# A fused attention and MLP kernel: attention of tiles 0 to 6 moved ahead of the first products with w_in

## The chip, the cores and the metric

The kernel runs on one core of a Trainium2 chip. The time is that of one execution on the device in microseconds (us); for a kernel several runs are taken and their median is given. Four engines compute: TensorE (PE in the profile, its weight loads PEld), VectorE (DVE), ScalarE (ACT) and GpSimd (POOL). SyncE (SP) only issues transfers. POOL issues those transfers that convert float32 to bfloat16 on the way.

## The reference

Attention with a band of 96 keys and 8 global keys, over 4 batches, 8 heads, 768 positions and a head size of 64; then an MLP with a squared ReLU on its 3072 rows of 512:

```python
scores = scale * np.matmul(q, k.transpose(0, 1, 3, 2))
is_global = pos[None, :] < n_global                  # 8
is_local = (rel >= 0) & (rel < n_local)              # 96
scores = scores - slopes * dist                      # per head
scores = np.where(is_global | is_local, scores, -1000000000.0)
a = np.exp(scores - np.max(scores, axis=-1, keepdims=True))
a = a / (np.sum(a, axis=-1, keepdims=True) + 1e-09)
x = np.matmul(a, v)                                  # heads joined: 3072 x 512
h = x @ w_in                                         # 512 x 2048
g = np.maximum(h, 0.0) ** 2
return g @ w_out                                     # 2048 x 512
```

## The kernel before

**Tiles.** The 3072 rows are 24 tiles of 128, six to a batch. A query tile needs its own keys, those of the tile before, and the 8 global keys of its batch; the first tile of a batch (0, 6, 12, 18) needs only its own. Two tiles make a pair, or block; the MLP runs by blocks, 12 of them.

**Steps of a tile**, by the names that the order uses; the line is where most of a step's work is issued:

- `ld` or `load`: POOL's transfers of q, k and v. `gate` is a tiny write ahead of a load into a buffer used before.
- `tr`: PE transposes q (n = 0) or k (n = 1), line 506; `T`: a copy of that from PSUM to `qkT`. From tile 8 on a transposing DMA on SP's queue does both, and is then called `T` alone.
- `bias`: for tiles 0 to 2, PE adds the position bias, line 579. `sc`: the scores, line 599.
- `exp`: ScalarE's exponential, line 665; `mul`: VectorE multiplies by E, the exponential of the bias, from tile 3 on, line 690. For a batch's first tile it is E0, made on VectorE in two halves.
- `gk`, `gv`: the 8 global keys or values are copied beside a tile's own; `kl` is a copy of keys that serves instead of `gk` for some tiles. The next tile needs them.
- `pv`: the product with v, line 748, in two halves of four heads; `norm`: VectorE's reciprocal and scaling, lines 778 and 779.
- `trx`: PE transposes x, line 816; `xT`: the copy of that. From tile 8 on both are one transposing DMA.

**The MLP.** Blocks 0 and 1 compute h step by step (`s1`, line 1061): 256 of the 2048 hidden columns in a step, each followed by `relu` and `sq`. Step s needs the transfer `win.s`; steps 0 and 2 come in two halves. Block 0's product with w_out is `s2.0` (line 1339). All other products are done with seven half-size products in the place of eight: `h` (line 950) and `s2` (line 1212), whose sums of operands VectorE makes (`isum`, `xs`, `wsum`, `sum`), and whose parts ScalarE and VectorE copy out and add (`u`, `c`, `q`, `part`, `o`). `u` is a copy of a partial result, in one of four buffers.

**What sets the order.** The kernel builds a list of all steps, with what each depends on, and a table of words, ORDER, gives the order in which they are issued. Every engine runs its own instructions strictly in that order. In a word, `@V`, `@A` and `@P` choose VectorE, ScalarE or POOL, the digits behind a colon name the PSUM banks (there are eight), and `#2` is the second piece of a step. The table is all that decides the order: the planner's estimates that stand in the code are not used when it runs.

**The start.** PE first runs eight products of zeros (line 372), then ORDER begins. Its second word is `warm`: eight more products of zeros, line 532, between the two transposes of tile 0:

```python
            def emit_warm(e):
                for _ in range(NKEEP):
                    nc.tensor.matmul(out=psum(), lhsT=zero[:, :P], rhs=zero, start=True, stop=True)
```

Tile 0's q and k come as float32 by SP; POOL loads the rest. In ORDER's first rows attention of tiles 0 to 3 comes ahead of the first `s1`; that of tiles 4 and 5 is spread among the products of blocks 0 and 1, and tile 6 follows after the first `h`.

Of the kernel before, what the change touches and what calls it, by code (L numbers as in the profile page):

```python
# [62 lines left out]
exp.3.0.1 T.1.4@V xT.1@V pv.2.1:0 ld.k.5 ld.win.2.0 exp.3.1.1 gk.3@A ld.win.2.1 norm.2.0 s1.0.3:2 mul.3.0 s1.0.6:4
ld.win.4.0 tr.0.4:7 ld.q.5 ld.v.4 norm.2.1 mul.3.1 relu.0.6@A s1.0.3#2 gv.2@P pv.3.0:3 norm.3.0 trx.2:5 T.0.4@A
pv.3.1:6 ld.win.1.0 norm.3.1 ld.win.0.1 xT.2@A sc.4.0:1047 exp.4.1.1 exp.4.1.0 tr.1.5:3 T.1.5@A s1.0.2:5 trx.3:6
xT.3@V ld.win.0.0 ld.win.5.0 s1.0.2#2 s1.0.2#3 s1.0.2#4 relu.0.3@V exp.4.0.1 ld.v.5 gv.3@P exp.4.0.0 gk.4@V sq.0.6@V
relu.0.2@A s1.1.3:7 ld.win.7.0 relu.1.3@A load.6 s1.1.6:0 mul.4.1 tr.0.5:6 mul.4.0 sq.0.3@V s1.1.2:3 T.0.5@A ld.wout.3
# [10 lines left out]
isum.1.0 T.8 s2.0.6.1 u.2.1.2@A s2.0.6.0 isum.3.0 pv.6.1:0 h.2.0.p6 wsum.2.1 wsum.0.1 s2.1.p1.1 s2.0.7.1 c.2.1.c11
norm.6.0 gate.13 o.0.1@V st.0.1 s2.0.7.0 h.2.1.p7 part.1.p1@A s2.1.p6.0 u.2.0.2@A o.0.0@A u.2.1.3@A h.2.0.p7 h.2.1.p4
T.9 norm.6.1 wsum.3.0 u.2.0.3@A sc.7.0:1762 c.2.1.c21@A wsum.1.1 h.2.1.p5:0 c.2.1.c22 q.2.1.c11@A s2.1.p2.0:4  # L80
exp.7.1.0 exp.7.0.0 isum.2.1 load.10 h.2.0.p4 exp.7.0.1 mul.7.0 exp.7.1.1 s2.1.p2.1 isum.2.0 s2.2.p1.0:7 q.2.1.c21@A
mul.7.1 h.2.0.p5:1 s2.1.p6.1 part.1.p6@A trx.6:6 gate.12 c.2.0.c21@A load.12 pv.7.0:2 xT.6@A c.2.0.c22 q.2.1.c22@A
q.2.0.c22@A s2.2.p1.1 h.2.1.p3 s2.1.p7.0 wsum.3.1 o.1.p2 norm.7.0 h.2.0.p3 pv.7.1:5 s2.1.p7.1 q.2.0.c21@A st.0.0
c.2.1.c12 s2.1.p5.0 s2.1.p5.1 part.1.p7@A q.2.1.c12@A s2.1.p4.0 T.10 s2.1.p4.1 c.2.0.c12 gk.7@V q.2.0.c12@A o.1.p5
o.1.p4@A sc.8.0:6201 st.1.1 part.2.p1@A s2.1.p3.0 norm.7.1 sum.2.0 sum.2.1 s2.1.p3.1 trx.7:5 xT.7@V o.1.p3 h.3.0.p1:3
exp.8.1.0 gk.8@V h.3.1.p1:2 exp.8.0.0 exp.8.1.1 exp.8.0.1 h.3.0.p2:6 xs.3.0 u.3.1.1@A sc.9.0:1540 s2.2.p6.0 mul.8.0
xs.3.1 mul.8.1 u.3.0.1@A h.3.0.p6 exp.9.0.1 exp.9.1.1 gv.7@V h.3.1.p2:4 c.3.0.c11 h.3.1.p6 c.3.1.c11 exp.9.0.0
pv.8.0:0 s2.2.p6.1 pv.8.1:6 load.11 norm.8.0 u.3.1.2@A s2.2.p2.0:1 sum.2.2 gv.8@P q.3.1.c11@A norm.8.1 xT.8 h.3.1.p7
h.3.0.p5:4 u.3.0.2@A h.3.0.p7 s2.2.p2.1 exp.9.1.0 st.1.0 part.2.p6@A xs.3.2 u.3.1.3@A q.3.0.c11@A h.3.1.p5:0 s2.2.p7.0
u.3.0.3@A mul.9.1 mul.9.0 s2.2.p7.1 c.3.1.c22 T.12 c.3.0.c22 pv.9.0:6 h.3.1.p3 o.2.p2 h.3.0.p4 c.3.1.c12 load.15  # L90
norm.9.0 q.3.1.c22@A h.3.0.p3 s2.3.p1.0:5 s2.3.p1.1 c.3.0.c12 q.3.0.c22@A pv.9.1:0 c.3.0.c21@A part.2.p7@A norm.9.1
q.3.1.c12@A h.3.1.p4 q.3.0.c12@A h.4.0.p1:3 c.3.1.c21@A s2.2.p5.0 part.3.p1@A gk.9@V sc.10.0:6402 s2.2.p5.1
q.3.0.c21@A sum.3.0 sum.3.1 s2.2.p4.0 s2.2.p4.1 exp.10.1.0 sum.2.3 exp.10.0.0 exp.10.0.1 h.4.0.p2:4 T.11 u.4.0.1@A
exp.10.1.1 gk.10@V gv.9@A s2.3.p6.0 o.2.p5 mul.10.0 c.4.0.c11 xT.9 h.4.1.p1:6 o.2.p4@A mul.10.1 s2.2.p3.0 s2.2.p3.1
q.3.1.c21@A s2.3.p2.0:0 sum.3.2 u.4.1.1@A pv.10.0:2 pv.10.1:4 s2.3.p6.1 xs.4.0 gate.17 o.2.p3 part.3.p6@A xs.4.1
s2.3.p2.1 norm.10.0 h.4.0.p6 h.4.1.p6 q.4.0.c11@A gv.10@A norm.10.1 u.4.0.2@A load.13 s2.3.p7.0 sc.11.0:7124 u.4.1.2@A
sum.3.3 h.4.0.p7 h.4.1.p7 xs.4.2 exp.11.1.0 o.3.p2 exp.11.0.0 u.4.0.3@V s2.3.p7.1 sc.12.0:17 exp.11.1.1 exp.11.0.1
gate.16 xT.10 h.4.0.p4 c.4.0.c21@A mul.11.0 st.2.0 mul.11.1 h.4.1.p2:4 c.4.1.c11 exp.12.1.0 s2.3.p5.0 pv.11.0:2
pv.11.1:3 s2.3.p5.1 norm.11.0 part.3.p7@A h.4.0.p5:7 q.4.1.c11@A u.4.1.3@A norm.11.1 h.4.1.p5:4 q.4.0.c21@A gate.20
s2.3.p4.0 c.4.0.c22 load.14 s2.3.p4.1 h.4.0.p3 T.13 gate.18 load.16 c.4.1.c22 exp.12.0.0 h.4.1.p4 q.4.1.c22@A h.4.1.p3  # L100
xT.11 s2.4.p2.0:2 h.5.0.p1:3 q.4.0.c22@A o.3.p5 mul.12.0 c.4.0.c12 o.3.p4@A c.4.1.c21@A u.5.0.1@A c.4.1.c12 T.15
s2.3.p3.0 q.4.0.c12@A s2.3.p3.1 q.4.1.c12@V q.4.1.c21@A h.5.0.p2:1 o.3.p3 sc.13.0:5764 st.3.1 st.2.1 h.5.1.p1:0
exp.13.0.0 T.14 s2.4.p2.1 c.5.0.c11 exp.13.1.0 pv.12.1:1 q.5.0.c11@A s2.4.p1.0:5 xs.5.0 sum.4.0 pv.12.0:7 xs.5.1
s2.4.p1.1 mul.13.0 h.5.0.p6 gk.13@V u.5.1.1@A exp.13.0.1 h.5.1.p6 exp.13.1.1 h.5.0.p5:6 sum.4.1 norm.12.0 norm.12.1
h.5.1.p2:4 xs.5.2 mul.13.1 c.5.1.c11 h.5.1.p5:7 u.5.1.2@A sum.4.2 gate.19 part.4.p1@A h.5.1.p7 u.5.0.2@A h.5.0.p7
o.4.p2 u.5.0.3@A c.5.0.c22 pv.13.0:1 u.5.1.3@A norm.13.0 s2.4.p6.0 s2.4.p6.1 xT.12 st.3.0 q.5.1.c11@A T.16 part.4.p6@A
h.5.0.p4 pv.13.1:4 s2.4.p5.0 sum.4.3 c.5.0.c21@A h.5.0.p3 h.5.1.p4 q.5.0.c22@A s2.4.p7.0 norm.13.1 s2.4.p7.1 s2.4.p5.1
c.5.0.c12 q.5.0.c21@A kl.15@V part.4.p7@A c.5.1.c22 q.5.0.c12@A sc.14.0:1346 o.4.p5 s2.4.p4.0 xT.13 exp.14.0.1 kl.14@V
h.5.1.p3 gv.13@P q.5.1.c22@V c.5.1.c12 c.5.1.c21@A s2.4.p4.1 load.17 h.6.0.p1:4 s2.4.p3.0 s2.4.p3.1 exp.14.1.1
exp.14.1.0 exp.14.0.0 sc.15.0:0673 mul.14.1 mul.14.0 xs.6.0 o.4.p4@A xs.6.1 h.6.0.p2:1 o.4.p3 q.5.1.c12@A s2.5.p1.0:5  # L110
u.6.0.1@A c.6.0.c11 exp.15.0.0 exp.15.1.0 exp.15.1.1 sum.5.0 s2.5.p1.1 h.6.0.p6 u.6.0.2@A exp.15.0.1 sum.5.1 load.18
h.6.0.p5:2 part.5.p1@A pv.14.0:0 norm.14.0 pv.14.1:6 h.6.1.p1:1 u.6.1.1@A h.6.0.p7 gv.14@P st.4.0 s2.5.p6.0 u.6.0.3@A
# [52 lines left out]
def kernel(  # L165
# [119 lines left out]
    HALVES = ((NBLK - 2, 0), (NBLK - 2, 1))  # L285
# [1146 lines left out]
```

## Time and profile before

| | |
|---|---|
| runs | 199.08, 199.46, 200.98 us; median 199.46 |
| profiled execution | 198.44 us, of which its span, first to last instruction, is 196.7 |
| PE busy | 190.8 us, 97% of the span, 2776 matmuls |
| VectorE, ScalarE, POOL busy | 173.9 (88%), 162.9 (83%), 80.9 (41%) |
| granted TensorE clock | 0.998 |

The profile records one execution. A row of a timeline gives start, length, engine, line and operands; of the chain of waits, start, length and what was running on the chain that ended last. A stretch's row gives the stretch, then the busy time of PE, PEld, DVE, ACT and POOL in it with the number of instructions, then the granted clock, the transfers' share and their rate. Lines of groups give busy time, mean length of one and idle time before.

Matmuls overlap, and so do other instructions at their ends; where one follows the other without a pause, the time from start to start is what an instruction costs its engine.

### The profile page before, as it was taken

The numbers are of one execution on the slowest core, as the hardware profiler recorded it, in microseconds if no ns is written. First come the engines' busy times: TensorE is split into PE (matmuls) and PEld (weight loads), VectorE is DVE, ScalarE is ACT, GpSimd is POOL, SyncE is SP. The second block draws the span as 40 slices with busy tenths as digits, with TensorE's granted clock in tenths as the row PEclk, the third lists the DMA queues.
The fourth block names the chain that finished last, engine by engine and source line by source line (L and its number), as shares of the span: only waits on it lengthen the run. The fifth ranks groups of instructions, "written<-read, shape, count | busy, mean of one in ns | idle before, by whom it ended". The sixth has DMA issues, their size and how long they took to land.

```text
span 196.7 us, 6776 instructions
## 1 busy us (share of the span) xinstructions
PE 190.8 (97%) x2776; PEld 169.0 (86%) x2776; DVE 173.9 (88%) x423; ACT 162.9 (83%) x335; POOL 80.9 (41%) x101
## 2 busy tenths in 40 slices
PE   7989999999999999999999999999999999999993
PEld 3678989767989989899989989989899989999992
DVE  8259879899999999799999999999899999989872
ACT  6579989966999898989889998998989879764750
POOL 8999998586018329312293803080400001000000
PEclk9999999999999999999999999999999999999999
DMA  8999999999999999999999999999796911114023
GB/s 131 146 170 167 181 182 185 181 202 158 158 187 182 108 198 104 158 166 207 174 110 191 111 131 188 170 107 108 117 76 130 143 53 57 30 27 163 0 107 107
DMA packets 111856, 26.91 MB, mean 137 GB/s; under 512 B 103378, under 2 KB 109010, under 8 KB 111826
## 3 DMA queue, kind: packets, MB, share of 16 engines
q0 software_dynamic: 80256, 13.37, 91.4%
q1 hardware_dynamic: 31570, 13.11, 32.4%
q8 instruction: 21, 0.34, 0.7%
q14 instruction: 9, 0.07, 0.1%
HBM read 27.26 MB, written 6.29 MB: 171 GB/s over the span
## 4 chain that ended last, share of the span: by engine, by line
PE 95%; DVE 3%; issue 1%; ACT 0%; DVEq 0%
PE bank L1212 35%; PE bank L950 32%; PE bank L1061 7%; PE bank L599 6%; PE bank L748 5%; PE bank L1339 4%; PE bank L372 2%; PE bank L506 2%; DVE qkT L433 1%; PE bank L532 1%; PE bank L816 1%; PE bank L579 0%; DVE v L433 0%; ACT qkT L429 0%; DVE o L1287 0%
## 5 line engine op out<-in xcount | busy, mean ns | idle before, releaser
L1015 ACT ACTIVATE hs<-hr 128x512 bf16<-128x512 f32 x72 | 44.8, 641 | 5.1 <-DVE hr L995 4.7
L665 ACT ACTIVATE esc<-bank 128x512 bf16<-128x512 f32 x78 | 42.9, 613 | 1.0 <-PE bank L599 0.7
L1212 PE MATMUL bank<-wsum,hsum 128*128 128x256 bf16 x264 | 36.2, 273 | 0.0
L1212 PEld LDWEIGHTS <-hsum 128*128 128x128 bf16 x360 | 32.1, 98 | 4.1 <-issue 0.5
L995 DVE CUSTOM_DVE_ANT_0 hr<-bank,early 128x512 f32<-128x512 f32 x45 | 30.4, 685 | 2.3 <-PE bank L950 1.5
L950 PEld LDWEIGHTS <-win 128*128 128x128 bf16 x480 | 29.7, 98 | 1.0
L950 PEld LDWEIGHTS <-qk_first 128*128 128x128 bf16 x480 | 29.7, 98 | 1.0
L429 ACT COPY early<-bank 128x512 f32<-128x512 f32 x42 | 24.5, 591 | 3.6 <-PE bank L950 3.3
L690 DVE TENSOR_TENSOR at<-esc,E 128x1024 bf16<-128x1024 bf16 x39 | 27.1, 705 | 0.1
L1212 PEld LDWEIGHTS <-hs 128*128 128x128 bf16 x264 | 24.0, 98 | 2.6
L310 POOL DMA_DIRECT2D qk<-in_q_dram x18 | 16.0, 888 | 23.3 <-DMA qkT<-qk 21.9
L1212 PE MATMUL bank<-wout,hs 128*128 128x256 bf16 x176 | 24.8, 273 | 0.0
L950 PE MATMUL bank<-xT,win 128*128 128x128 bf16 x320 | 23.4, 219 | 0.0
L310 POOL DMA_DIRECT2D v<-in_v_dram x18 | 16.0, 889 | 18.0 <-DVE v L480 14.1
L431 POOL COPY v<-v 8x520 bf16<-8x520 bf16 x8 | 6.1, 760 | 41.3 <-PE bank L748 41.3
L950 PE MATMUL bank<-xs,qk_first 128*128 128x128 bf16 x320 | 22.8, 219 | 0.0
L779 DVE TENSOR_TENSOR x<-bank,rs 128x256 bf16<-128x256 f32 x48 | 20.4, 424 | 1.7
L865 ACT ACTIVATE hr<-bank 128x512 f32<-128x512 f32 x33 | 19.4, 599 | 1.9 <-DVE hs L1100 0.8
L748 PE MATMUL bank<-v,at 128*128 128x65 bf16 x352 | 17.8, 193 | 0.2 <-DVE v L433 0.2
L1287 DVE TENSOR_TENSOR o<-bank,part 128x256 f32<-128x256 f32 (+2 forms) x34 | 13.8, 410 | 3.3 <-PE bank L1212 3.2
L429 ACT COPY part<-bank 128x256 f32<-128x256 f32 x29 | 10.9, 375 | 7.0 <-PE bank L1212 6.9
L748 PEld LDWEIGHTS <-at 128*128 128x128 bf16 x352 | 15.2, 98 | 1.3 <-issue 0.3
(92 smaller groups left out, 365.8 us busy)
## 6 DMA issues: line engine op xcount, KB each, us to landing
out_dram<-o SPq DMA_DIRECT2D x22, 256.0 KB, 2.5
v<-in_v_dram POOLq DMA_DIRECT2D x24, 128.0 KB, 5.3
qk<-in_q_dram POOLq DMA_DIRECT2D x18, 128.0 KB, 5.0
qk<-in_k_dram POOLq DMA_DIRECT2D x18, 128.0 KB, 5.1
wout<-in_moe_w_out_dram POOLq DMA_DIRECT2D x8, 256.0 KB, 8.5
win<-in_moe_w_in_dram POOLq DMA_DIRECT2D x6, 256.0 KB, 6.8
qk_first<-in_k_dram POOLq DMA_DIRECT2D x5, 128.0 KB, 4.5
qk_first<-in_q_dram POOLq DMA_DIRECT2D x5, 128.0 KB, 5.8
```

Source lines behind the costliest of these rows:

```text
L310: nc.gpsimd.dma_start(out=dst, in_=src)
L429: nc.scalar.copy(dst, src)
L665: nc.scalar.activation(out=tiles[tag, j, g][:, odd], in_=tiles.pop(("sc", j, odd, g)).rearrange("p a c -> p (a c)"), func=Act.Exp, scale=s ...
L690: nc.vector.tensor_mul(at, tiles.pop(("esc", j, g)), bias)
L748: nc.tensor.matmul(out=po[:, hi, :], lhsT=tiles["at", j, g][:, odd, at * P : (at + 1) * P], rhs=v_sb[kj][:, h, :], start=(i == 0), stop=(i ...
L779: nc.vector.tensor_tensor(out=x[:, 4 * hf : 4 * hf + 4, :], in0=po[:, :, :D], in1=rs.to_broadcast([P, 4, D]), op=Alu.mult,)
L865: nc.scalar.activation(dst, src, Act.Relu)
L950: nc.tensor.matmul(out=tiles["h", blk, g, bank][:, n], lhsT=left_[:, s, k], rhs=right_[:, k], start=opens and n == 0 and k == 0, stop=k == ...
L995: nc.vector._custom_dve(TENSOR_ADD_SAT, out=hr, in0=src, in1=tiles.pop(("u", blk, g, i)), s0=float("inf"), s1=0.0,)
L1015: nc.scalar.activation(hs, hr, Act.Square)
L1212: nc.tensor.matmul(out=tiles["acc", blk, bank][:, cols], lhsT=left_[:, s], rhs=right_[:, cols], start=first and s == 0, stop=s == NSTEP - ...
L1287: nc.vector.tensor_tensor(out=o_sb[:, cols], in0=tiles["acc", blk, bank][:, part], in1=tiles["part", blk, other][:, part], op=Alu.add,)
```

## The change

The table is written anew up to tile 21, and from tile 22 on only the bank numbers and the place of a few stores differ. The eight zero products behind tile 0's first transpose are gone. POOL's loads come at the head of the table in an order of their own: q, k and v of tiles 0 to 5, with those of tile 6 in between, and of w_in nothing ahead of tile 3's values; most of it behind tile 5's keys and queries. Attention of tiles 0 to 6 now stands ahead of the first `s1`, but for the last products of tiles 4 and 5. Loads 8 and 9 come after all of w_out. Some copies change engine.

Three small edits go with it. Steps joined in one word may take their banks one behind the other (`at`). The output product names the landing of the previous tile's values as a dependency of the planner. The four `u` buffers are taken from a list of free ones and not in turn.

```diff
 ORDER = """
-tr.0.0:0 warm:7 tr.1.0:1 T.1.0@V bias.0.0:23 T.0.0@A sc.0.0 exp.0.0.0 ld.k.1 tr.1.1:4 bias.1.0:5670 T.1.1@V ld.q.1
-tr.0.1:1 ld.v.0 exp.0.1.0 T.0.1@V sc.1.0 exp.1.0.1 pv.0.0:2 ld.q.2 tr.0.2:3 norm.0.0 ld.k.2 T.0.2@V ld.k.3 exp.1.1.1
...
+ld.k.2 ld.k.1 ld.q.1 ld.q.2 ld.v.0 tr.0.0:0 ones.6 load.6 ld.v.1 ld.k.3 ld.q.3 ld.v.2 ld.k.5 ld.q.4 ld.q.5 ld.k.4
+ld.v.3 ld.win.6.0 ld.win.1.0 ld.v.4 ld.win.4.0 ld.win.2.1 ld.win.2.0 ld.v.5 ld.win.0.0 ld.win.0.1 load.7 ld.win.3.0
...
-    NKEEP = 8
...
-        if j == 0:
-            def emit_warm(e):
-                for _ in range(NKEEP):
-                    nc.tensor.matmul(out=psum(), lhsT=zero[:, :P], rhs=zero, start=True, stop=True)
-
-            plan.op(("warm",), {"PE": 0.216 * NKEEP}, emit_warm, key=base)
...
-        def open_sc(gs, j=j):
-            for n, (g, odd) in enumerate((g, odd) for g in gs for odd in range(2)):
+        def open_sc(gs, at=0, j=j):
+            for n, (g, odd) in enumerate(((g, odd) for g in gs for odd in range(2)), at):
...
-                deps.append(glob.get(("v", j - 1)))
+                deps += [glob.get(("v", j - 1)), land["v", j - 1]]
...
-    u_next = [0]
+    u_free = list(u_ring)
...
-                    u = u_ring[u_next[0] % NU]
-                    u_next[0] += 1
+                    u = u_free.pop(0)
...
+                        u_free.append(u)
```

Two places show how rows move. The first is POOL's queue, where transfers are issued one after the other. Before, these are its first ones (`qk_first` holds q and k of tiles 1 to 5, `v_71` to `v_76` the values of tiles 0 to 5); the first part of w_in is eighth, the second twelfth:

```order
L307 DMA qk_first<-in_k_dram 128x8x64
L307 DMA qk_first<-in_q_dram 128x8x64
L307 DMA v_71<-in_v_dram 128x8x64
L307 DMA qk_first<-in_q_dram 128x8x64
L307 DMA qk_first<-in_k_dram 128x8x64 x2
L307 DMA v_72<-in_v_dram 128x8x64
L307 DMA win<-in_moe_w_in_dram 128x4x256
L307 DMA qk_first<-in_q_dram 128x8x64
L307 DMA qk_first<-in_k_dram 128x8x64
L307 DMA v_73<-in_v_dram 128x8x64
L307 DMA win<-in_moe_w_in_dram 128x4x256
```

After, eleven transfers of tiles stand ahead of these rows (q, k of tiles 1, 2 and 3, the values of tiles 0 and 1, and tile 6):

```order
L306 DMA v_73<-in_v_dram 128x8x64
L306 DMA qk_first<-in_k_dram 128x8x64
L306 DMA qk_first<-in_q_dram 128x8x64 x2
L306 DMA qk_first<-in_k_dram 128x8x64
L306 DMA v_74<-in_v_dram 128x8x64
L306 DMA win<-in_moe_w_in_dram 128x4x256 x2
L306 DMA v_75<-in_v_dram 128x8x64
L306 DMA win<-in_moe_w_in_dram 128x4x256
L306 DMA win<-in_moe_w_in_dram 128x4x128 x2
L306 DMA v_76<-in_v_dram 128x8x64
L306 DMA win<-in_moe_w_in_dram 128x4x128 x2
```

The first part of w_in, that of step 6, has moved from the eighth to the eighteenth place, behind the values of tile 3.

The second place is VectorE's list ahead of its first `relu` (the row that writes `hr`). Before, two products with E of tile 3 (L690) and the norms of tiles 2 and 3 (L778 and L779) stand there, and one copy of x:

```order
L690 TENSOR_TENSOR at<-esc,E 128x1024
L778 RECIPROCAL rs<-bank_107 128x4
L779 TENSOR_TENSOR x<-bank_107,rs 128x256
L690 TENSOR_TENSOR at<-esc,E 128x1024
L778 RECIPROCAL rs<-bank_110 128x4
L779 TENSOR_TENSOR x<-bank_110,rs 128x256
L778 RECIPROCAL rs<-bank_113 128x4
L779 TENSOR_TENSOR x<-bank_113,rs 128x256
L433 COPY xT<-bank_113 128x4x128
L867 TENSOR_SCALAR hr<-bank_109 128x512
```

After, the same stretch of the list is tile 3's second product with E, the copies of tile 5's queries (`qkT_86`) and of tile 4's global keys (`qkT_85`), tile 3's two norms, both products with E of tile 4, and a copy of global values (`v_74`) ahead of the `relu`:

```order
L684 TENSOR_TENSOR at<-esc,E 128x1024
L432 COPY qkT_86<-bank_113 128x512
L432 COPY qkT_85<-qkT_81 128x4x8
L772 RECIPROCAL rs<-bank_108 128x4
L773 TENSOR_TENSOR x<-bank_108,rs 128x256
L772 RECIPROCAL rs<-bank_111 128x4
L773 TENSOR_TENSOR x<-bank_111,rs 128x256
L684 TENSOR_TENSOR at<-esc,E 128x1024 x2
L432 COPY xT<-bank_109 128x4x128
L432 COPY v_74<-v_71 8x8x65
L861 TENSOR_SCALAR hr<-bank_112 128x512
```

Tile 4's products with E and the global values of tile 3 have moved ahead of the first `relu`; the scores of tile 5 need the rows down to `qkT_85`, and the output products of tile 4 need the copy into `v_74`.

More of the change, by code (lines that the diff above doesn't have):

```diff
@@ L63 @@
[L63 to L67, printed above, removed]
@@ L78 @@
[L78 to L82, printed above, removed]
@@ L83 @@
[L83 to L112, printed above, removed]
@@ new lines @@
+q.2.1.c21@A h.3.0.p7 u.3.0.3@A o.1.p2 sc.8.0:4651 exp.8.0.0 s2.1.p7.1 s2.1.p5.0 h.3.0.p5:4 exp.8.1.0 xs.3.2 c.2.1.c12
+h.3.0.p4 part.1.p7@A sum.1.3 gk.8@V wsum.3.1 exp.8.1.1 exp.8.0.1 s2.1.p5.1 h.3.1.p1:2 q.3.0.c11@V c.3.0.c22
+q.2.1.c12@A mul.8.1 c.3.0.c21@A h.3.0.p3 sc.9.0:6150 s2.1.p4.0 sum.2.0 u.3.1.1@A mul.8.0 c.3.0.c12 s2.1.p4.1 exp.9.1.0
+o.1.p5 h.3.1.p6 q.3.0.c21@A pv.8.0:1 pv.8.1:4 exp.9.0.1 norm.8.0 norm.8.1 exp.9.0.0 s2.1.p3.0 s2.1.p3.1 exp.9.1.1
+mul.9.1 h.3.1.p2:5 o.1.p3 xT.8 st.1.0 st.0.0 T.13 o.1.p4@A gk.9@A u.3.1.2@A gv.8@A sc.10.0:6107 exp.10.0.1 mul.9.0
@@ new lines @@
+exp.10.0.0 s2.2.p1.0:4 h.3.1.p7 u.3.1.3@A exp.10.1.1 sum.2.1 sum.2.2 q.3.0.c22@A h.3.1.p5:3 c.3.1.c22 s2.2.p1.1
+pv.9.1:0 part.2.p1@V mul.10.1 pv.9.0:6 h.3.1.p4 norm.9.0 s2.2.p2.0:7 s2.2.p6.0 s2.2.p6.1 gate.18 c.3.1.c11 exp.10.1.0
+q.3.0.c12@A s2.2.p2.1 h.3.1.p3 norm.9.1 gk.10@A part.2.p6@A s2.2.p7.0 xT.9 st.1.1 c.3.1.c12 sc.11.0:1650 sum.2.3
+q.3.1.c11@A q.3.1.c22@A exp.11.0.0 gv.9@V exp.11.1.0 mul.10.0 s2.3.p1.0:3 s2.3.p1.1 c.3.1.c21@A o.2.p2 part.3.p1@V
+mul.11.0 s2.2.p7.1 exp.11.1.1 part.2.p7@A q.3.1.c12@A exp.11.0.1 pv.10.1:1 pv.10.0:6 h.4.0.p1:2 gv.10@V norm.10.0
@@ new lines @@
+h.10.0.p7 q.10.0.c11@V exp.23.0.1 exp.23.1.1 s2.9.p6.0 u.10.0.3@A xs.10.2 pv.22.0:6 pv.22.1:4 gv.22@P norm.22.0
+norm.22.1 h.10.1.p6 exp.23.1.0 u.10.1.2@A h.10.0.p5:1 s2.9.p2.0:6 exp.23.0.0 h.10.0.p4 h.10.1.p7 sum.9.2 s2.9.p2.1
+q.10.1.c11@A s2.9.p6.1 c.10.0.c22 mul.23.1 h.10.0.p3 mul.23.0 o.9.p2 h.10.1.p5:5 q.10.0.c22@A part.9.p6@A u.10.1.3@A
+pv.23.1:4 pv.23.0:7 c.10.1.c22 norm.23.0 s2.9.p7.0 s2.9.p7.1 norm.23.1 part.9.p7@V h.10.1.p3 s2.9.p5.0 s2.9.p5.1
+q.10.1.c22@A o.9.p5 c.10.0.c21@A s2.10.p1.0:7 s2.10.p1.1 q.10.0.c21@A xT.22 h.10.1.p4 c.10.0.c12 q.10.0.c12@A
@@ L994, in emit_c @@
                     if i:
[L995 to L997 removed]
+                        u = tiles.pop(("u", blk, g, i))
+                        nc.vector._custom_dve(TENSOR_ADD_SAT, out=hr, in0=src, in1=u, s0=float("inf"), s1=0.0)
+                        u_free.append(u)
                     else:
```

155 lines of the change are left out of this document (89 added, 66 removed).

## The prediction

> **What bounds the kernel now.** I read the busy times by stretch first, then the waits of PE, then the chain of waits at the start.
>
> ```profile
> 20.00:25.00 5.00, 5.00 (x77) 4.41 (x74) 4.31 (x10) 4.53 (x9) 5.00 (x7) 1.00 1.86 180
> ...
> 100.00:110.00 10.00, 10.00 (x167) 8.99 (x162) 9.83 (x25) 9.47 (x21) 6.52 (x9) 1.00 1.81 148
> ```
> ```profile
> PE bank L372 <- DVE early L361: 1.2, 1, 1.2
> PE bank L599 <- DVE qkT L433: 1.1, 3, 0.5
> PE bank L1212 <- DVE o L1287: 0.5, 1, 0.5
> PE bank L748 <- DVE v L433: 0.2, 1, 0.2
> ```
>
> In the stretches the columns behind the first two are PE, PEld, DVE, ACT and POOL. PE (TensorE) is the bound: from 20 us on it is busy in every microsecond of a stretch (two of the rows are shown), and in the whole span its waits add up to 3.0 us. The rest of the span is matmuls, and the change leaves these as they are, eight zero products excepted. So the time after is the time before, less the zeros, plus or minus PE's idle time. Where idle time can change shows in the chain's first 20 us (start, length, what):
>
> ```profile
> 1.19 3.60 PE bank L372 x8
> 4.79 0.46 PE bank L506 x4
> 5.25 1.73 PE bank L532 x8
> ...
> 8.20 0.40 PE bank L599 x8
> 8.60 0.33 PE bank L506 x4
> 8.93 0.87 PE bank L579 x8
> ...
> 10.54 0.62 PE bank L599 x16
> ...
> 17.41 1.32 PE bank L1061 x16
> 18.73 0.22 PE bank L506 x4
> 18.95 0.45 PE bank L1061 x8
> 19.40 0.24 PE bank L748 x8
> ```
>
> **Zeros: -1.73 us of PE, and their cover.** L532 is the eight zero products. Without them the bound could fall by 1.73 us at most, if real work stood ready there. The next steps count by one yardstick: from 5.25 us to the first product with w_in (L1061), how much of PE's time was attention, and how much was lost.
>
> Before, these groups stand there: the key transpose of tile 0, 0.45; biases 0.44 (half of 0.87, by its width) and twice 0.87; seven bf16 transposes of 0.22; scores 0.40 and three times 0.62; output products (L748) of tiles 0, 1 and 2, 0.24 and four times 0.24; two transposes of x, as long as others, 0.22. That is 8.1 us. The first product starts at 17.41, so 17.41 - 5.25 - 8.1 = **4.1 us are lost**, 1.7 of them zeros.
>
> After, PE's list has all of tiles 0, 1, 2, 6 and 3, scores of 4 and 5, and only then the first product (step 6): 0.45, biases 2.18, twelve transposes 2.64, scores 2 x 0.40 + 5 x 0.62, output products 1.9, three transposes of x 0.66: **11.8 us**. With no wait the first product would start at 17.0. Two things decide when it really does.
>
> **w_in's landing.** POOL issues the loads one after the other:
>
> ```profile
> 1.34 1.01 POOL L307 DMA_DIRECT2D qk_first<-in_k_dram  x1 [0.17 <-issue]
> 2.35 0.88 POOL L307 DMA_DIRECT2D qk_first<-in_q_dram  x1
> ```
> ```profile
> DMA to landing us min/median/max: 5.7/6.7/7.3
> ```
>
> The second answer is that of w_in's loads. Step 6 of w_in is eighteenth after the change, so it is issued at 1.34 + 1.01 + 16 x 0.88 = 16.4 us and lands between 22.1 and 23.7. The 1.9 to 4.5 us that PE has nothing to multiply lie beside attention's own waits, below, and are not added to them.
>
> **VectorE and ScalarE.** Running seven tiles at once asks these two for more than PE can hide. Their rows at the start, in which one instruction follows the other without a pause, give the pace as start to start:
>
> ```profile
> 8.63 1.08 ACT L665 ACTIVATE at<-bank 128x512 bf16<-128x512 f32 x2 [2.29 <-PE bank L599]
> ...
> 16.24 2.11 ACT L665 ACTIVATE esc<-bank 128x512 bf16<-128x512 f32 x4
> 18.15 0.30 ACT L429 COPY qkT<-qkT 128x32 bf16<-128x32 bf16 x1
> ```
> ```profile
> 15.99 0.76 DVE L433 COPY v<-v 8x520 bf16<-8x520 bf16 x1
> 16.66 0.40 DVE L433 COPY qkT<-bank 128x512 bf16<-128x512 bf16 x1
> 16.99 0.40 DVE L433 COPY xT<-bank 128x512 bf16<-128x512 bf16 x1
> 17.32 0.16 DVE L778 RECIPROCAL rs<-bank 128x4 f32<-128x4 f32 x1
> 17.52 0.42 DVE L779 TENSOR_TENSOR x<-bank,rs 128x256 bf16<-128x256 f32 x1
> 17.86 0.68 DVE L690 TENSOR_TENSOR at<-esc,E 128x1024 bf16<-128x1024 bf16 x1
> 18.46 0.17 DVE L778 RECIPROCAL rs<-bank 128x4 f32<-128x4 f32 x1
> ```
>
> An exponential costs ScalarE (18.15 - 16.24) / 4 = 0.48. On VectorE a copy of transposes costs 0.33, a norm (L778 and L779) 0.54, a product with E 0.60, a copy of global values 0.67; one of global keys I put at the 0.30 of ScalarE's at 18.15.
>
> The first exponential stays near 8.63: the zeros go, but VectorE now makes both casts of tile 0 with half of E0 between them. Behind it ScalarE has exponential, exponential, tile 1's keys: 3 x 0.48, and the keys are there 0.6 after their start, at 10.2. Only then do tile 1's scores run. Exponential again 0.43 after that (8.63 - 8.20), at 10.7; two of them and the global keys to 11.9; tile 2's scores to 12.6; the output product behind them; and norm.0.1 starts 0.4 later, near 13.1. From there VectorE's list to the scores of tile 5 has 7 norms (3.8), 5 copies of transposes and one of xT (2.0), 3 products with E (1.8), 2 copies of global values (1.3) and 2 of global keys (0.6): 9.5 us without a gap, to 22.6. Scores of tile 5, 0.62: the first product starts at **23.2**. That is inside w_in's landing, so the two limits nearly coincide. Lost then are 23.2 - 5.25 - 11.8 = 6.2 us, **2.1 more than before**, zeros counted.
>
> **Just behind it.** The output products of tile 4 wait for gv.3, which VectorE reaches after 2 norms, 2 products with E, an xT and the copy itself: 22.6 + 1.1 + 1.2 + 0.3 + 0.7 = 25.9. Ahead of them PE has two products with w_in of 0.9 (twice the row at 18.95) and two transposes of x, 2.2, to 25.4. **0.5 us** lost. The next products with w_in and their relus are queued behind on PE, all ready.
>
> **From 40 us on.** The order moves work to VectorE: over the program 8 more copies of global values, 6 relus, 4 squares, 3 copies u, 4 copies of transposes; it takes away 4 copies of global keys, 2 kl, 2 squares and 2 xT. Behind the first product of tile pair 1 with w_out, 5 of those copies, the 4 squares, the 3 u and a part stay, less 4 keys and 2 kl.
>
> ```profile
> 42.00:166.00 124.00, 124.00 (x1915) 112.39 (x1912) 117.87 (x275) 112.30 (x233) 42.11 (x50) 1.00 1.32 142
> ```
> ```profile
> L433 DVE COPY v<-v 8x520 bf16<-8x520 bf16 x4 | 1.9, 486 | 0.0
> L1017 DVE TENSOR_TENSOR hs<-hr 128x512 bf16<-128x512 f32 x8 | 5.5, 686 | 0.1
> ```
>
> These are 5 x 0.49, 7 x 0.69 and 0.4, less some 2.0 for the small copies: about 5.7 us, onto a VectorE that is idle for 6.1 of 124 us. Bounds: nothing, since the stretch 100 to 110 has VectorE at 9.83 of 10 and PE at 10.00; and 5.7, if VectorE keeps its idle share and becomes the bound. I take **1.2**, nearer to that row.
>
> **What costs nothing.** The bookkeeping of banks and u buffers and the new dependency of output products are the planner's own: the order is fixed by the table. POOL makes three copies instead of eight, which only frees its queue for loads. Ahead of the loads of tiles 8 and 9 stand the same transfers in both orders, so these two still land near 51.
>
> ```profile
> 51.23 2.12 SPq L537 DMA_TRANSPOSE qkT<-qk  x1
> ```
> ```profile
> qkT<-qk SPq DMA_TRANSPOSE x16, 3.8
> ```
>
> So the first transposing DMA still starts near 51. It is tile 9's now, tile 8's is queued behind it on SP and lands near 57, and tile 8's scores stand near 59.7 (58.2 before, 1.1 us less real work ahead, 2.6 us more lost). Cover 2.7 us; beyond it each microsecond of lateness is one of PE. The end, from tile 22 on, differs only in banks.
>
> **Sum.** 2.1 + 0.5 + 1.2 = 3.8 us on the profiled execution's 198.44 us (span 196.7) is 202.2. The median shown is 199.46, 1.0 above that execution; the forecast for a median is 199.46 + 3.8 = **203.3 us**.
>
> **Rivals.** (1) Data alone sets the start: the two engines find overlaps that my in-line sum doesn't have, and the first product starts when w_in lands at the earliest, 22.1. Lost 5.0, 0.9 more than before, nothing later: **200.4**. For it: the limits lie 1.1 us apart. Against: VectorE's list is in order and has no gap to close. Chance 0.17.
>
> (2) Faster: the first product finds its data early and the zeros' 1.73 us is won. From a start at 21.1 us nothing is lost against before; for a gain of 1% it must start by 19.1, and with no wait at all 17.0 gives 199.46 - 4.1 = **195.4**. Against: 19.1 asks that w_in lands 2.7 us after its issue, while the shortest above took 5.7. Chance 0.05.
>
> (3) VectorE becomes the bound from 40 on: 2.1 + 0.5 + 5.7, **207.8**. For it: 117.87 of 124. Against: PE at 10.00 beside 9.83. Chance 0.10.
>
> (4) The clock falls in the thin start. The same 128x512 products took 3.60 us for eight at first and 1.73 us later (rows at 1.19 and 5.25), so PE starts at half its pace; if it fell back at the end of the attention, eight such products' time would cost 1.9 us again: **205.2**. PE would be at work for 11.8 of the 18 us from 5.25 to 23.2, with no single wait over 1.5. Chance 0.06. The Trainium skill, "TensorE: Matmul & The Clock Gate" (What's actually happening), says that an idle window of about 3.4 us throttles the clock to half and a busy one releases it; by that rule the zeros' removal is a risk only if a whole window is empty, and no row of before shows one.
>
> **How the numbers follow.** The forecast's case has 0.62, with 201.5 to 205.5 as its own range. Of the cases, 200.3 to 207 leaves out the gain, the upper part of (3) and little else. A measurement here tells no change from about 1%, 197.5 to 201.5: faster 0.05; within, (1) and the forecast's low edge, 0.22; slower 0.73.
>
> **What would show it.** In the profile after: the first product with w_in at about 23 us; VectorE at 5.00 of 5 from 15 to 20 and nearly so to 25; PE below 3.5 of 5 there; the chain of the start through VectorE and ScalarE instead of PE; waits of PE for VectorE's global values near 26; hardly any wait in 40 to 166. A first product before 21 us, or PE waiting for tile 8's or 11's transposes, would prove me wrong.

## The result, and the profile after

| | before | after |
|---|---|---|
| median of 20 runs each, on the same chip | 199.51 us (198.52 to 200.98) | 202.63 us (200.30 to 204.76) |
| ratio after to before | | 1.0105, interval 1.0073 to 1.0136 |
| profiled execution, its span | 198.44, 196.7 us | 201.55, 199.8 us |

The kernel after is slower by 3.1 us in the medians and in the two profiled executions, by 2.1 us in the ratio, which leaves out six runs of after that lie over 1.5% above its fastest. 203.3 was predicted, with a range of 200.3 to 207.0.

The page's head, and busy time by stretch (PE, PEld, DVE, ACT, POOL, then the clock, the transfers' share and their rate), with one row of the kernel before last:

```profile
PE 190.8 (95%) x2764; PEld 169.2 (85%) x2768; DVE 180.5 (90%) x437; ACT 157.0 (79%) x326; POOL 77.0 (39%) x96
```
```profile
15.00:20.00 5.00, 3.92 (x77) 3.29 (x78) 4.65 (x16) 4.80 (x12) 5.00 (x7) 1.00 2.19 156
20.00:25.00 5.00, 4.04 (x78) 3.35 (x76) 4.90 (x15) 4.11 (x8) 4.25 (x7) 1.00 1.67 185
25.00:30.00 5.00, 5.00 (x74) 4.64 (x71) 4.46 (x13) 3.31 (x7) 4.54 (x6) 1.00 2.14 163
100.00:110.00 10.00, 10.00 (x160) 9.36 (x159) 9.48 (x23) 8.72 (x20) 1.23 (x2) 1.00 1.62 156
42.00:166.00 124.00, 123.67 (x1831) 110.97 (x1832) 118.45 (x271) 104.08 (x218) 40.62 (x47) 1.00 1.37 141
```
```profile
15.00:20.00 5.00, 4.55 (x90) 4.13 (x88) 4.86 (x19) 4.62 (x11) 4.91 (x8) 1.00 2.04 168
```

PE has the same work as before without the zeros, so the time was lost where PE is below full. That is the start, up to 25 us, with VectorE at 4.65 and 4.90 of 5 (before, it was as busy from 15 to 20, but at 4.31 from 20 to 25); from 25 us on PE is nearly as full as it was. The waits of PE (total, times, longest):

```profile
PE bank L593 <- ACT qkT L428: 2.1, 3, 1.1
PE bank L505 <- DMA qk_first<-in_k_dram: 1.5, 2, 0.8
PE bank L371 <- DVE early L360: 1.2, 1, 1.2
PE bank L1205 <- DVE o L1280: 0.4, 1, 0.4
PE bank L742 <- DVE at L684: 0.4, 1, 0.4
```

The waits for ScalarE's copies of keys, which the scores (L593) need, and for the first transfers (L505) are new. The chain of waits up to the first product with w_in (L1054; start, length, what):

```profile
9.41 1.07 ACT at L659 x2
10.49 0.49 ACT qkT L428
10.97 0.05 issue
11.02 0.42 PE bank L593 x8
...
16.71 0.69 DVE at L684
...
20.10 0.60 DVE at L684
20.70 0.40 DVE v L432
...
21.21 0.36 DVE x L773
21.57 0.68 DVE at L684
22.25 0.05 issue
22.29 0.42 PE bank L742 x8
22.71 0.65 PE bank L593 x16
23.36 0.98 PE bank L1054 x8
```

Ahead of these rows it begins with the landing of tile 2's keys, at 6.38. It runs through ScalarE, then VectorE from 16.7 us without a gap: product with E, copy of global values, norm, product with E. Then come tile 3's output product, tile 5's scores, and the first product at 23.3 us.

To compare kernels I worked PE's idle time out of the trace: each matmul's start-to-start time less the median of the same pair of shapes over these kernels, summed by stretch (gaps that are missing records left out). The zeros, 1.73 us, are counted as idle here. In us:

```
                    to 30 us   30 to 60   60 to 180
before                6.53       0.46       2.64
before_no_zeros       6.05       1.48       4.01
before_packed         7.38       0.46       3.33
before_fill           6.45       1.23       3.36
after                 8.73       0.34       3.70
after_zeros           8.72       0.46       2.75
after_early           8.72       0.34       3.14
after_less_vector     8.31       0.50       3.24
after_w_late          9.32       0.27       4.27
after_gv_twice        8.00       0.34       7.23
```

Between the two profiles the start makes 8.73 - 6.53 = 2.2 us, and the part behind 60 us 1.06. The first is there, with 1.5 to 2.8 us, in every kernel with the start of after. The second isn't: four profiles with the later order of before have 2.64 to 4.01, and five with that of after 2.75 to 4.27.

### The profile page after: what moved, and what is told of

It reads as the page before. It is cut to its first block, busy times and chain, and to the rows that moved or that the text cites. A ratio compares the mean times of both kernels' runs of the same rounds, so it can differ in the third digit from the quotient of the medians.

```text
span 199.8 us, 6761 instructions
## 1 busy us (share of the span) xinstructions
PE 190.8 (95%) x2764; PEld 169.2 (85%) x2768; DVE 180.5 (90%) x437; ACT 157.0 (79%) x326; POOL 77.0 (39%) x96
## 4 chain that ended last, share of the span: by engine, by line
PE 77%; DVE 8%; DMA 6%; ACT 6%; issue 2%; POOL 0%; POOLq 0%; ACTq 0%
PE bank L1205 30%; PE bank L944 27%; PE bank L1054 7%; PE bank L593 5%; PE bank L742 4%; DMA xT<-x 3%; PE bank L1332 3%; DMA qk_first<-in_k_dram 3%; ACT at L659 2%; DVE at L684 2%; DVE hr L989 2%; ACT esc L659 2%; DVE x L773 1%; ACT hs L1008 1%; DVE o L1280 1%
## 5 line engine op out<-in xcount | busy, mean ns | idle before, releaser
L1008 ACT ACTIVATE hs<-hr 128x512 bf16<-128x512 f32 x68 | 42.0, 635 | 9.1 <-DVE hr L989 8.6
L659 ACT ACTIVATE esc<-bank 128x512 bf16<-128x512 f32 x78 | 44.0, 610 | 4.6 <-PE bank L593 3.4
L1205 PEld LDWEIGHTS <-hsum 128*128 128x128 bf16 x360 | 32.8, 98 | 4.5 <-issue 0.7
L989 DVE CUSTOM_DVE_ANT_0 hr<-bank,early 128x512 f32<-128x512 f32 x43 | 29.2, 683 | 2.4 <-PE bank L944 2.2
L684 DVE TENSOR_TENSOR at<-esc,E 128x1024 bf16<-128x1024 bf16 x39 | 26.2, 680 | 0.4 <-ACT esc L659 0.4
L428 ACT COPY early<-bank 128x512 f32<-128x512 f32 x40 | 23.4, 592 | 2.1 <-PE bank L944 1.9
L944 PE MATMUL bank<-xs,qk_first 128*128 128x128 bf16 x320 | 23.2, 219 | 0.0
L859 ACT ACTIVATE hr<-bank 128x512 f32<-128x512 f32 x27 | 16.1, 600 | 2.6 <-PE bank L1054 1.4
L309 POOL DMA_DIRECT2D qk<-in_k_dram x18 | 16.2, 899 | 1.1 <-issue 0.7
L430 POOL COPY v<-v 8x520 bf16<-8x520 bf16 x3 | 1.9, 617 | 36.6 <-PE bank L742 36.6
L1054 PE MATMUL bank<-xT,win 128*128 128x256 bf16 (+1 forms) x160 | 15.9, 251 | 0.0
```

The lines of the kernel that those rows point to most:

```text
L309: nc.gpsimd.dma_start(out=dst, in_=src)
L428: nc.scalar.copy(dst, src)
L659: nc.scalar.activation(out=tiles[tag, j, g][:, odd], in_=tiles.pop(("sc", j, odd, g)).rearrange("p a c -> p (a c)"), func=Act.Exp, scale=s ...
L684: nc.vector.tensor_mul(at, tiles.pop(("esc", j, g)), bias)
L859: nc.scalar.activation(dst, src, Act.Relu)
L944: nc.tensor.matmul(out=tiles["h", blk, g, bank][:, n], lhsT=left_[:, s, k], rhs=right_[:, k], start=opens and n == 0 and k == 0, stop=k == ...
```

## The experiments

Every run stands beside runs of the kernel before on the same chip; kernels of different experiments are compared by their ratios to it. That of after is 1.0105.

**Zeros out of the kernel before.** `before_no_zeros`:

```diff
-tr.0.0:0 warm:7 tr.1.0:1 T.1.0@V ...
+tr.0.0:0 tr.1.0:1 T.1.0@V ...
```

> The kernel before, without its eight zero products and nothing else. Theory (the zeros stand where PE would soon wait for loads anyway): PE is ahead by 1.7 us at tile 0 and loses it again at tile 4's keys, which landed at 14.93 us; the first product with w_in starts at about 16.9 instead of 17.3, and the time falls by 0.3 to 0.6 us. Rival (the zeros are PE time like any other): 1.7 us less. Rival (the zeros hold the clock): slower, with half-rate products behind tile 0.

Measured: 199.54 beside 199.61, ratio 1.0005 (0.9983 to 1.0026): no gain, neither the 1.7 us nor, as far as the runs can tell, the 0.3 to 0.6. The first product starts 1.45 us sooner, at 15.80, but tile 6's scores are no sooner (37.85 beside 37.66). The chain shows why; PE waits for tile 6's keys:

```profile
25.66 7.82 DMA qk<-in_k_dram
33.48 0.05 issue
33.52 0.40 PE bank L506 x4
```

Without the zeros the start of before goes at the pace of its loads up to this point; the zeros lay in time that the loads gave away.

**Zeros put back into the kernel after.** `after_zeros` has the word `warm:7` again, behind `tr.0.0:0`.

> The changed kernel with the eight zero products put back behind tile 0's first transpose. Theory: PE waits there for tile 2's keys until 6.43 us anyway, so 1.15 of the 1.73 us are covered; the rest moves tile 0's scores by up to 0.6, and the first product with w_in by 0 to 0.6 us. Rival (zeros cost their full time): 1.7 us more. Rival (without zeros PE's clock suffers): faster than the changed kernel.

Measured: 202.47 (ratio 1.0157, 1.0123 to 1.0192), with the first product at 23.28, as without them, and the same idle time up to 30 us with the zeros counted: in the trace they cost nothing there either. The runs alone don't settle it: the median is 0.2 us below that of after, the ratio 0.005 above, and the intervals overlap only just.

**The start of after, begun earlier.** `after_early`: tile 0's scores no longer wait for tile 2's keys in PE's list, nor its copy behind half of E0.

```diff
-... tr.1.2:1
-tr.1.0:2 bias.0.0:34 T.0.0@V E0.1 T.1.0@V tr.1.1:5 T.1.2@V gate.9 bias.1.0:6702 tr.0.1:1 sc.0.0 exp.0.0.0 T.0.1@V
-tr.0.2:1 T.0.2@V exp.0.1.0 T.1.1@A ...
+tr.1.0:2 bias.0.0:34 T.0.0@V T.1.0@V tr.1.2:1 sc.0.0 tr.1.1:5 exp.0.0.0 T.1.2@V gate.9 bias.1.0:6702 tr.0.1:1 T.0.1@V
+tr.0.2:1 T.0.2@V E0.1 exp.0.1.0 T.1.1@A ...
```

> The changed kernel, with PE's and VectorE's first steps in another order: tile 0's key transpose, its bias and its scores come ahead of the transposes of tiles 1 and 2, and the first half of E0 behind the copies of tile 2. Tile 1's scores then run near 9.3 instead of 11.0 us; loads keep their order. Theory (the in-line work of ScalarE and VectorE sets the start): the first product with w_in moves from 23.3 to about 22.2, where w_in lands, and the time falls by about 1.1 us. Rival (the tile loads set it, tile 4's keys at 19.5 last): no change of the first product, within 0.3 us.

Measured: 201.31 (ratio 1.0108, 1.0064 to 1.0151). Scores of tiles 0 and 1 are 1.45 and 0.85 us sooner, at 7.52 and 10.17. The first product stays at 23.28. Its chain begins with the landing of tile 1's values, at 13.21, and ends as that of after does:

```profile
8.41 4.80 DMA v<-in_v_dram
13.21 0.05 issue
13.25 0.43 PE bank L742 x8
...
21.54 0.69 DVE at L684
22.23 0.05 issue
22.28 0.42 PE bank L742 x8
22.70 0.65 PE bank L593 x16
```

So the theory failed and the rival held, with tile 1's values in the place of tile 4's keys. In this execution the earlier head is lost again: VectorE's list cannot go on before tile 1's values are there, and from there its longest gap is 0.27 us. The ratio is that of after.

**w_in later still.** `after_w_late` loads the values of tiles 4 and 5 ahead of step 6 of w_in.

```diff
-ld.v.3 ld.win.6.0 ld.win.1.0 ld.v.4 ld.win.4.0 ld.win.2.1 ld.win.2.0 ld.v.5 ...
+ld.v.3 ld.v.4 ld.v.5 ld.win.6.0 ld.win.1.0 ld.win.4.0 ld.win.2.1 ld.win.2.0 ...
```

> The changed kernel, with the values of tiles 4 and 5 loaded ahead of the first parts of w_in: step 6 of w_in lands at about 23.9 instead of 22.2 us, all else as it was. Theory (work, not w_in, sets the first product): it moves from 23.3 to 24.0 at most, 0 to 0.7 us more. Rival (w_in's landing sets it): the full 1.7 us more.

Measured: 202.30 (ratio 1.0158, 1.0115 to 1.0200). The landing has moved from 22.20 to 23.82, and the first product from 23.3 to 23.87:

```profile
18.04 5.78 DMA win<-in_moe_w_in_dram
23.82 0.05 issue
23.87 1.05 PE bank L1054 x8
```

In the profile of after w_in landed 1.1 us ahead of the first product; here PE waited 1.15 us for it, so the work ahead was done near 22.7. The two limits lie 0.5 to 1.1 us apart. (In POOL's queue of before, the eighth transfer is the part for step 3; that for step 6 is the twelfth.)

**VectorE's list shorter.** `after_less_vector`:

```diff
+                if j <= 6:
+                    nc.vector.tensor_copy(x[:, 4 * hf : 4 * hf + 4, :], po[:, :, :D])
+                    return
                 nc.vector.reciprocal(rs, po[:, :, D : D + 1])
...
-                any_copy(e, v_sb[j][:n_global], v_sb[j - t][:n_global])
+                if j not in (1, 2):
+                    any_copy(e, v_sb[j][:n_global], v_sb[j - t][:n_global])
```

> The kernel after, with VectorE's list of the start made shorter: the output of tiles 0 to 6 is not divided by the row sums (no reciprocal, a copy in the place of the product), and the global values are not copied to tiles 1 and 2. What sets the first product with w_in? Theory 1 (VectorE's list): ahead of the scores of tile 5 five to seven reciprocals of 0.16 to 0.2 us and copies of 0.28 to 0.48 are gone, so the list ends at least 1.1 us sooner and the first product starts where its data land, 22.2 to 22.5 instead of 23.3; the time falls by about 1 us, to 201.6 beside 202.6 of the kernel after. Theory 2 (the loads of v1 and k4 pace the start): the first product stays at 23.2 to 23.4, and so does the time.

Measured: 201.25 (ratio 1.0113, 1.0068 to 1.0158); first product at 22.46. VectorE now has gaps at 15.7 and 18.9 us, and PE waits for w_in instead (page of waits):

```profile
PE bank L1058 <- DMA win<-in_moe_w_in_dram: 0.2, 1, 0.2
```

That is what theory 1 had in the trace, w_in's landing as the next limit. The microsecond that it had in the time isn't shown: the ratio is that of after, 1.0105, within its interval. Nor is the size in the trace shown by this run alone: with the start of after unchanged, the first product stood at 23.3 in two profiles (`after`, `start_of_after`) and at 22.55 in two others (`after_gv_pool`, `after_gv_twice`), where the chain was VectorE's as well. Of the 0.8 us between 23.3 and 22.46, up to 0.75 can be this spread.

**Global values copied by POOL.** `after_gv_pool` turns `gv.9@V`, and so those of tiles 10, 13, 14, 15 and 16, to `@P`.

> The kernel after, with the copies of global values of tiles 9, 10, 13, 14, 15 and 16 made on POOL instead of VectorE. It asks whether VectorE's extra work from 40 us on is the 1 us that the steady part lost. Theory 1 (VectorE's load): six copies of 0.49 us leave it, and 0.5 to 1 us comes back: about 201.8, with the first product still at 23.3. Rival (the loss comes from the order of the work, not from that load): 202.4 to 202.8, no change.

Measured: 220.43 us (ratio 1.107, 1.1038 to 1.1103), outside both expectations; it says nothing on VectorE. One copy stands in POOL's queue behind loads that wait for a transposing transfer, and PE waits for the copy (first the wait of PE, then POOL's rows with the idle time ahead in brackets):

```profile
PE bank L742 <- POOL v L430: 15.6, 2, 12.8
```
```profile
108.89 0.88 POOL L309 DMA_DIRECT2D qk<-in_q_dram  x1 [9.61 <-DMA qkT<-qk]
109.76 0.89 POOL L309 DMA_DIRECT2D qk<-in_k_dram  x1
...
113.22 0.62 POOL L430 COPY v<-v 8x520 bf16<-8x520 bf16 x1
```

The copy takes 0.62 us, PE's wait for it 12.8.

**Before, with the engines of after.** `before_engines` keeps the order of before and changes the letter behind `@` in 35 words from tile 7 on, among them two copies of global values that come to POOL.

> The kernel before, its order kept, but with the engines that the kernel after chooses for 35 steps from tile 7 on (copies of global keys and values, u, q, part, o). The start is that of before. If the choice of engines makes the loss of the steady part: before plus 0.8 to 1.2, 200.3 to 200.8. If the order of the work makes it: before plus or minus 0.3.

Measured: 214.65 us (ratio 1.0768, 1.0734 to 1.0801). It is outside both expectations. One wait goes back to POOL's queue: a copy of global values that waits 10.1 us for output products ends at 145.5, behind it come the loads, behind these the transposes, and PE waits for them for 4.5 us at once. That is less than a third of the 15 us lost, and POOL's copies wait as long in all in the kernel before (41.3 us, here 40.7); the rest, spread over many shorter waits, wasn't followed. Engines and order of a table belong together, and this run doesn't separate them.

**Loads of before, re-ordered.** `before_packed` loads tile 3's queries and tile 4's keys ahead of w_in's first part, step 6 of w_in ahead of tile 2's values, and tile 6's keys first of its three. It has no zeros.

```diff
-pv.0.1:4 tr.1.2:1 bias.2.0:7203 ld.v.1 ld.win.3.0 norm.0.1 exp.1.1.0 ld.q.3 tr.1.3:6 ...
+pv.0.1:4 tr.1.2:1 bias.2.0:7203 ld.v.1 ld.q.3 ld.k.4 norm.0.1 exp.1.1.0 tr.1.3:6 ...
...
-T.1.3@V ld.k.4 pv.1.0:4 ld.v.2 gk.2@V ...
+T.1.3@V ld.win.3.0 ld.win.6.0 pv.1.0:4 ld.v.2 gk.2@V ...
```

> The kernel before without the zeros of its second word, and with the loads re-ordered to what PE waited for in that kernel: keys of tile 4 and queries of tile 3 ahead of the first part of w_in, the part for step 6 ahead of tile 2's values, and tile 6's keys ahead of its queries and values. If the pace and order of the loads is what hid the zeros' removal: the waits at 14.2 (0.36), 16.9 (0.62) and 33.5 us (0.67) go, the scores of tile 6 start near 36.2 instead of 37.7 to 37.9, and the time falls by 1.2 to 1.6 us, to 198.0 to 198.4. If another engine takes over as soon as the data are there (VectorE, as in the kernel after): 199.2 to 199.6, no gain.

Measured: 200.16 beside 199.33 (ratio 1.0051, 1.0023 to 1.0079), a microsecond slower and outside both expectations. I had overlooked that tile 2's output products stand ahead of the first product with w_in; their values now land at 17.6 and PE waits for them:

```profile
PE bank L745 <- DMA v<-in_v_dram: 1.8, 1, 1.8
```

The wait for tile 6's keys went, 0.46 us idle in 30 to 60 us instead of 1.48.

**Two of before's gaps filled.** `before_fill` has no zeros, puts the second piece of the first product with w_in (`s1.0.3#2`) ahead of the one that waits for step 6, and loads tile 6's keys first.

> The kernel before without the zeros of its second word, and with two changes at places where PE waited in that kernel: the second piece of the first product with w_in (0.6 us, its data there) stands ahead of the product that waits for step 6 of w_in, and tile 6's keys are loaded ahead of its values. If the loads' pace is what gave the zeros' gain back, these two waits of 0.62 and 0.67 us go: 198.3 to 198.9. If another wait takes their place: 199.2 to 199.8.

Measured: 199.39 beside 199.59 (ratio 0.9989, 0.9961 to 1.0016). Both waits went, and others stand in their place: at 16.0 the 0.4 us for a copy of global values that the kernel before has at 16.8, and 0.55 us, new, at 31.9 for another copy, which POOL makes behind loads:

```profile
31.85 0.37 PE L747 MATMUL bank<-v,at 128*128 128x65 bf16 x7 [0.39 <-POOL v L431]
```

No version here beats the kernel before by more than the measurement can tell.

**VectorE's small copies doubled.** `after_gv_twice`:

```diff
                 any_copy(e, v_sb[j][:n_global], v_sb[j - t][:n_global])
+                if j >= 9 and e == "DVE":
+                    any_copy(e, v_sb[j][:n_global], v_sb[j - t][:n_global])
```

> The kernel after, with every copy of global values that VectorE makes from tile 9 on made twice: some 3 us more for VectorE behind 60 us. It doubles the suspected cost. Theory 1 (VectorE has room there): 202.0 to 203.0, as the kernel after. Theory 2 (VectorE is as good as the bound, so that five such copies cost the 1 us): 203.6 or more, since seven more of 0.3 to 0.5 us are added.

Measured: 203.81 (ratio 1.0197, 1.0144 to 1.0250). The group of these copies grew from the first row to the second, by 2.7 us:

```profile
L432 DVE COPY v<-v 8x520 bf16<-8x520 bf16 x12 | 4.7, 390 | 0.0
```
```profile
L432 DVE COPY v<-v 8x520 bf16<-8x520 bf16 x19 | 7.4, 390 | 0.2
```

The median is 1.2 us above that of after. The ratio is 0.0092 above, or 1.8 us, and by the two intervals 0.6 to 3.0; so VectorE's added time came through in part, by the middle of this estimate in two thirds, and VectorE has little room behind 60 us. In the profile one wait of 1.4 us at 81.7 stands out. It is for a transposing transfer of x that landed 8.04 us after its issue, where the median of its kind was 3.4; that the copies cause it isn't shown.

**Starts and rests exchanged.** `start_of_after` has the first 430 words of after and the rest of before; `rest_of_after` the first words of before and the rest of after. With the rests joined in this way some buffers are used in another order, so that part of the output is made of other tiles' data; the instructions are the same.

> The first 430 words of the order after, which reach to about 70 us (tile 10's scores), and behind them what is left, in the order and with the engines of before. Theory 1 (the whole loss lies in the start): before plus 1.8 to 2.4, 201.3 to 201.9, and behind 80 us no loss against before. Theory 2 (the steady part of the order after loses about 1 us more, as the two profiles have it): the same 1.8 to 2.4, which is then 1 us less than the kernel after. It is the pair with the next kernel that tells them apart.

Measured: 203.68 (ratio 1.0197, 1.0149 to 1.0245).

> The first words of the order before, without its zeros, up to about 70 us, and behind them what is left, in the order and with the engines of the kernel after. Theory 1 (the whole loss lies in the start): the time of before, 199.2 to 199.8. Theory 2 (VectorE is fuller behind 40 us, or the order there is worse, and 1 us is lost): 200.2 to 200.8.

Measured: 213.89 (ratio 1.0711, 1.0658 to 1.0763). Both lose time at the joint, between 60 and 100 us, so the pair doesn't decide on the steady part. In the first, PE waits there for sums of x (3.4 us by the page), behind a transfer of 8.18 us:

```profile
75.16 8.18 DMA xT<-x
...
83.43 0.43 DVE xs L915
```

What it does show: the start of after lost the same in it (first product at 23.30). Between 100 and 180 us its PE idles for about 2 us; kernels of either order lie between 1.5 and 2.6 there, so that stretch doesn't tell them apart.

## Why the prediction was right, and where not

**The start, 2.1 us: right in size and place.** Measured 2.2, with the first product at 23.3 against 23.2. The chain goes through ScalarE and then VectorE as said. w_in's step 6 landed at 22.20, inside 22.1 to 23.7, and `after_w_late` and `after_less_vector` show that the two limits lie within about 1 us: the chain through VectorE's list is the later one, w_in the next. That the list alone sets the time isn't shown, since the kernel with the shorter list is no faster by its ratio. (The 1.9 to 4.5 us given beside w_in's landing don't follow from its own times: 22.1 and 23.7 less 17.0 are 5.1 and 6.7. Nothing was added up from them.)

**Errors inside it cancelled, which is luck.** The first exponential was to stay near 8.63; it came at 9.40. Tile 2's keys are the first transfer of POOL, and PE's first step after tile 0's queries needs them: they landed at 6.38 and PE waited 0.8 us. I had priced the transposes as if they came in the old order. Tile 1's scores came at 11.02 and not 10.2, and the second norm of tile 0 at 13.63 and not 13.1. On the other side copies of global values took 0.28 and 0.48 us instead of 0.67, and VectorE's list, with one gap of 0.16 us at 16.7, ended at 22.25, for 22.6 predicted. Behind it PE had tile 3's output product as well as the scores, 1.1 us in place of 0.62.

What the late head costs isn't settled. In `after_early` an earlier one bought nothing, since tile 1's values landed at 13.21. But in `after_gv_pool` and `after_gv_twice`, whose start is that of after, tile 2's keys landed at 5.8 and 5.7, the first exponential came at 8.84 and 9.05, and the first product stood at 22.55. So the moment at which the first keys land may make a part of the spread of 0.75 us, and small copies of other lengths the rest.

**Zeros: right.** Their cover was complete on both sides: no gain in time without them in before, no later first product with them in after.

**Tile 4's output products, 0.5 us: this step failed.** VectorE reached the copy at 25.19 and ended it in 0.28 us, when PE came at 25.51:

```profile
25.19 0.28 DVE L432 COPY v<-v 8x520 bf16<-8x520 bf16 x1
```
```profile
25.51 0.65 PE L742 MATMUL bank<-v,at 128*128 128x65 bf16 x16
```

The term that was mis-sized is the 0.67 of the copy, taken from one row of before; no wait was left.

**From 40 us on, 1.2 us: not shown.** VectorE was to have 5.7 us more there. Its busy time in 42 to 166 rose by 0.6 only (117.87 to 118.45), but that stretch misleads: the program after runs some 3 us later, and a part of its work falls behind 166. From 42 us to the end VectorE is busy for 144.9 us instead of 141.2, 3.6 more. PE's idle time behind 60 us was 1.06 us more in the two profiles, which comes near the 1.2, but profiles of either order differ among themselves by 1.4 and 1.5 us and their ranges are nearly the same. `after_gv_twice` gives an estimate of what a microsecond more on VectorE costs there, about 0.7 (1.8 us for 2.7, by the intervals 0.2 to 1.1); the prediction had 1.2 / 5.7 = 0.2. So the amount was too high and the price probably too low; what the two make together no run here shows.

**Tile 8's cover: right.** The first transposing transfers were issued at 52.03 (51 predicted), its scores stood at 59.14 (59.7 predicted), and PE waited for none.

**The sum.** 3.8 predicted; 3.1 measured in medians, 2.1 in the ratio. That 202.6 came so near to 203.3 is in part luck: of the three terms only the start is shown, and the long runs of after lift its median. The start accounts for 2.2 of it, and the ratio's 2.1 (1.5 to 2.7, the interval times 199.5) needs no more. The other 0.9 in the medians is **open**: the runs of after reach over 4.5 us, those of before over 2.5, and a profile shows only one of them. A part may lie in the start, whose first product came at 22.55 to 23.30 in kernels that begin as after does; why some runs take 204 us wasn't found.

**Signs that were to show it.** VectorE was at 4.65 and 4.90 of 5, a little less than said. PE was to be below 3.5 of 5 and was at 3.92 and 4.04. From start to start it idles for 2.0 and 1.7 us in these two stretches: the busy time of short products counts their overlap, so it hides waits that the starts show, and that sign was badly chosen. The wait for global values near 26 didn't come.

**Rivals.** The one that data alone sets the start was close, within a microsecond. VectorE as the bound from 40 on did not come: PE is busy for 123.67 of 124 us there. The clock's fall did not come either: the granted clock is 1.00 in the stretches of the start, where PE never waited much over 1 us. (For the first microseconds that column says nothing: it reads 1.00 from 0 to 5 us in the kernel before, where eight products ran at half pace.) A fall needs less than a whole empty window, though; what it takes is in the last section.

## What to carry to other kernels

Fillers like the zeros cost nothing here, where loads set the pace; ask what lands when before counting their removal as a gain. Work gathered at the front meets the in-order list of the engine that copies and scales: add that list up, instruction by instruction, and set its end beside the landing of the first weights. And before a small copy goes to an idle engine, read what waits ahead of it in that engine's queue: behind a POOL copy of 0.62 us PE waited 12.8, and the kernel lost 18 us.

## What the runs showed of the hardware

The clock in `after_gv_pool`, where PE stopped at 101.1 us and went on at 113.88:

```profile
102.00:103.00 1.00, 0.00 (x0) 0.00 (x0) 0.11 (x1) 0.97 (x3) 0.00 (x0) 1.00 1.58 279
103.00:104.00 1.00, 0.00 (x0) 0.00 (x0) 0.00 (x0) 0.60 (x2) 0.00 (x0) 0.83 2.27 169
104.00:105.00 1.00, 0.00 (x0) 0.00 (x0) 0.00 (x0) 0.00 (x0) 0.00 (x0) 0.50 1.95 159
...
116.00:117.00 1.00, 1.00 (x11) 0.94 (x10) 0.00 (x0) 0.00 (x0) 0.00 (x0) 0.50 0.34 34
117.00:118.00 1.00, 1.00 (x11) 0.87 (x10) 0.69 (x1) 0.00 (x0) 0.00 (x0) 0.84 0.00 0
118.00:119.00 1.00, 1.00 (x21) 0.95 (x20) 0.53 (x3) 0.88 (x3) 0.62 (x1) 1.00 0.00 0
```

With two levels, 1 and 0.5, the mean of 0.83 puts the fall at 103.7, 2.6 us after PE stopped, and that of 0.84 the return at 117.3, 3.4 us after it went on. So a wait of 12.8 us costs about half of another 3.4, an estimate from these rows. The Trainium skill, "TensorE: Matmul & The Clock Gate" (What's actually happening), gives a free-running window of about 3.4 us for both. The return agrees; the fall doesn't, since 2.6 us after PE stopped no window of that length had been empty as a whole, and the measurement decides.

`rest_of_after` shows the same. PE's waits up to there were 2.1 us at most, and the clock fell all the same, at 74.8 by the mean of 0.85:

```profile
72.00:76.00 4.00, 1.29 (x28) 1.20 (x30) 1.23 (x4) 2.76 (x8) 1.90 (x3) 0.85 0.50 53
76.00:80.00 4.00, 3.75 (x38) 3.14 (x35) 3.15 (x11) 2.47 (x5) 4.00 (x5) 0.50 1.82 116
```

Six such falls lie inside the runs here. In the 3.41 us ahead of each PE was busy for 0.2 to 1.3 us, and the clock stayed at half for 3.4, 6.8 or 13.7 us, multiples of one length. Behind such a stretch with 1.78 us of work (`before_engines`, 166.34 to 169.76) it did not fall. The emptiest one in the start of `after` has 2.3.

The copy of global values, the same instruction on 8 partitions, took 0.28 to 0.79 us on VectorE in these runs; a price from one row of it is worth little. And transposing transfers of x took 2.8 to 4.2 us in the median of a kernel; the longest took 5.2 to 6.4 in the five kernels with the order of before, and 7.0 to 8.9 in the nine that have the order of after in whole or in part.
